# Query, key and value products of chunks 1 and 2 of the first layer, computed during chunk 0's attention and kept in DRAM

## The chip, the cores and the metric

The kernel runs on one core of a Trainium2 chip. A core has TensorE (PE, with its weight loads PEld), VectorE (DVE), ScalarE (ACT), GpSimd (POOL) and SyncE (SP), each with an instruction queue of its own that it works through in order, and 16 DMA engines that all queues share. The metric is the device time of one launch in microseconds, the median of several runs.

## The reference, cut to what matters

Two layers follow each other on 2048 rows of 576 numbers; both use the same weights.

```python
def _A_ref(x, wqkv, wo):               # 32 heads of 18, window W = 8, dilation 2
    qkv = (x @ wqkv) ...               # q, k, v
    idx = pos[:, None] - arange(W) * 2 # each row looks at itself and 7 earlier rows, 2 apart
    logits = q . k[idx] * 18 ** -0.5   # masked where idx < 0
    o = softmax(logits) . v[idx]
    return o @ wo
def _B_ref(x, w1, w2):                 # 576 -> 4608 -> 576
    return silu(x @ w1) @ w2
for layer in range(2):
    x = x + _A_ref(layernorm(x), wqkv, wo)
    x = x + _B_ref(layernorm(x), w1, w2)
```

## The kernel before

The 2048 rows are cut into four chunks of 512 rows. A chunk takes the even or the odd rows (`par`) of one half (`blk`) of the sequence, so that a window lies within rows of one chunk and, for the second half, of the end of the chunk two before it. Within a chunk row 4p+j of it lies in partition p, tile j (NJ = 4 tiles of 128). A step s is one chunk of one layer: s = 0 to 3 are chunks 0 to 3 of layer 0, s = 4 to 7 those of layer 1.

All matrix products take both sides in two float16 halves, a high one and the rest. `passes` (L283) makes 14 matmuls of one product over 576 rows. `front(s)` (L744) makes what comes ahead of the feed-forward of a step:

- `load_x` (L733) loads four x tiles. `layer_norm` (L306) takes statistics on DVE (L311, L312), a Newton inverse root in some 14 small steps (L317 to L327), and scales: on DVE (L335, L340, L294) or, where `on_act` is set, partly on ACT (L343, L346). A DMA transpose on SP (L300) then puts the two halves of each tile into `xa` or `xb`, [128, 9, 512].
- `attention` (L452) goes through four units u of 8 heads. Per unit and tile j PE makes q, k and v at once, 128x432 (L476, called a tile below), and ACT copies them from the `misc` bank into `kv` and `qt` (L480, L482). Four DMAs on ACT's queue copy the halo (L491): the earlier rows that a partition's window needs lie in its neighbours. The edge of a first half is set to zero by POOL (L461, L462), that of a second half is fetched by SP from what POOL saved (L467, L496). DVE multiplies and reduces for the logits (L504, L508, two tiles at a time), does the softmax around the exponential on ACT (L516 to L524, L527), multiplies with the values (L537) and sums over the window (L544, L545).
- `project` (L549) splits o into halves (L558, L294), transposes it into `oT` (L300), multiplies with wo on PE (L573), and adds to x (L580). A second `layer_norm` fills `xb`.

`ffn(s)` (L668) takes the 36 column tiles f of w1. PE makes z (L696, 14 matmuls of 128x512, called a z tile), ACT applies silu and makes the high half of h (L698, L700), DVE the low half (L703). After a group of 6 (step 0) or 9 tiles PE multiplies h with w2 into `acc` (L714; 18 matmuls, called a group, per three f and row tile), and DVE adds it to x (L580).

In step 0 the weights come raw from DRAM: the wqkv columns of a unit (L369), wo (L417), w1 and w2 (L605 to L609), all issued by SP. ACT and DVE scale them and split them into halves (L391 and L394, L438 and L441, L640 to L647), and POOL stores the halves in DRAM (L398, L650, L652), from where later steps load them.

The order of the instructions is not that of the code. Each `op` is given to a planner (L50) with an engine, an assumed duration, the buffers that it needs and a priority; the planner goes through time, and whenever an engine is free it takes the ready operation with the lowest priority number whose buffers are free. Buffers come from tags with a fixed number of slots (L211 to L234), most of them handed out in the order in which the code asks. `after=gate[-1:]` holds the early loads back until chunk 0's first layer norm is done. The attention of a step has priority s - 1, its feed-forward products s + 0.5 and the work around them s - 0.5, so that the attention of step s + 1 is done on DVE and ACT while PE works on the feed-forward of step s. For chunk 0 there is no such feed-forward: its attention, and the splitting of the first weights, stand at the start of the program.

The shared buffer of z on PSUM has two banks, `misc` two, `acc` two.

Of the kernel before, what the change touches and what calls it, by code (L numbers as in the profile page):

```python
# [191 lines left out]
def sliding_attention_silu_ffn(ctx: ExitStack, tc: tile.TileContext, x, wqkv, wo, w1, w2, out):  # L192
# [15 lines left out]
    def T(b):  # L208
# [9 lines left out]
    tag("lg", 2, [P, NJ, W, UH], F32)  # L218
# [5 lines left out]
    tag("oT", 1, [P, 9, P], F16, turns=False)  # L224
    tag("w1", 6, [P, 10, P], F16)
    tag("w2", 11, [P, 2, D], F16)
    tag("h", 11, [P, 2, TB], F16)
    tag("hs", 2, [P, TB], F32)
# [12 lines left out]
           for l in range(NL) for p in range(2) for u in range(NU)}  # L241
# [61 lines left out]

    gate = []

    def layer_norm(xs, prio, into, on_act):  # L306
# [24 lines left out]
        for j in range(NJ):  # L331
# [29 lines left out]
    def raw_wq(u):  # L361
# [3 lines left out]
        for k in range(5):  # L365
# [9 lines left out]
            op("SP", 0.1, load, [], [rs[k]], -9 + u, nbytes=P * 3 * UC * 4, after=gate[-1:] if u > 1 else ())  # L375
# [32 lines left out]
    def raw_wo():  # L408
        rs = [Buf("w2") for _ in range(5)]
        p = -0.7  # L410
        for k in range(5):
# [9 lines left out]
            op("SP", 0.1, load, [], [rs[k]], p, nbytes=P * D * 4, after=gate[-1:])  # L421
# [30 lines left out]
    def attention(s, xT, wq):  # L452
# [4 lines left out]
        for u in range(NU):  # L457
            kv, qt, w = Buf("kv"), Buf("qt"), wq(u)
            if blk == 0:
                def clear(kv=kv):  # L460
                    nc.gpsimd.memset(T(kv)[0:2, 0:3], 0.0)  # L461
                    nc.gpsimd.memset(T(kv)[0:1, 3:7], 0.0)  # L462
                op("POOL", 1.6, clear, [], [(kv, "edge")], pr_)
            else:
# [4 lines left out]
                op("SP", 0.2, edge, [("eds", lay, par, u)], [(kv, "edge")], pr_, nbytes=20000)
            for j in range(NJ):  # L470
                m = Buf("misc")

                def mm(j=j, m=m, w=w):
                    pl = list(passes(lambda k: T(xT)[:, k, j * P:(j + 1) * P], lambda k: T(w)[:, k, :]))
                    for n, (a, b) in enumerate(pl):
                        nc.tensor.matmul(T(m)[:, :3 * UC], a, b, start=n == 0, stop=n == len(pl) - 1)  # L476

                def evac(j=j, m=m, u=u, kv=kv, qt=qt):
                    d = du[:, u:u + 1]
                    nc.scalar.activation(T(kv)[:, j + W - 1].rearrange("p a b -> p (a b)"), T(m)[:, UC:3 * UC],  # L480
                                         AF.Copy, scale=d)
                    nc.scalar.activation(T(qt)[:, j, :], T(m)[:, 0:UC], AF.Copy, scale=d)  # L482
                op("PE", 2.6 if s else 3.9, mm, [(xT, j)] + [(w, k) for k in range(10)], [m], pr_)
                op("ACT", 0.9, evac, [m, ("su", u)], [(kv, j), (qt, j)], pr_)

            def halo(kv=kv):
                t = T(kv)

                for p0, n, i, m in ((0, 112, 3, 4), (112, 15, 3, 4), (0, 112, 0, 3), (112, 14, 0, 3)):
                    d = 1 if i else 2  # L490
                    nc.scalar.dma_start(t[p0 + d:p0 + d + n, i:i + m], t[p0:p0 + n, 11 - m:11])  # L491
            own = [(kv, j) for j in range(NJ)]
            op("ACT", 2.4, halo, own, [(kv, "halo")], pr_ - 0.2, nbytes=P * 14 * UC * 4)
            if blk == 0:
                def save(kv=kv, u=u):
                    nc.gpsimd.dma_start(eds[lay, par, u], T(kv)[P - 2:P, 7:11].rearrange("p a b c -> p (a b c)"))  # L496
# [291 lines left out]
```

## Time and profile before

| | |
|---|---|
| median of 3 runs | 2324.41 us (2321.84 to 2326.78) |
| profiled execution | 2322.78 us |
| its span, first to last instruction | 2321.0 us |
| mean granted TensorE clock | 0.976 |
| busy: PE, DVE, ACT, POOL | 2183.4, 1412.3, 730.5, 96.5 us |
| DMA | 325.42 MB, mean 140 GB/s |
| first z of the program | 238.46 us |

The profile is one execution. Section 1 of its page gives busy time and the number of instructions of each engine, section 2 the same in 40 slices (each digit is the busy share in tenths), section 4 the chain of work that ended last, followed back from the end. A row of a group reads: line, engine, operation, tiles, shapes, count, then busy time in us, mean ns of one, and the idle time of the engine just before them with what ended it. The prediction also uses the chain in order of time (start, length, what), windows (busy time of each engine between two times) and the timeline (start, length, engine, line). A fence of the order shows instructions as they stand in the program on one engine, without times; a name such as kv_79 is one buffer.

### The profile page before, as it was taken

Reading aid. Unit: us, or ns where it says so; the run is one execution under the profiler, and the core shown is the slowest. Engines: PE = TensorE matmul, PEld = TensorE weight load, DVE = VectorE, ACT = ScalarE, POOL = GpSimd, SP = SyncE. Lnnn points to the kernel's source line nnn. Section 1 sums busy time; section 2 is a strip of 40 time slices with the busy share of each in tenths; the row PEclk is TensorE's granted clock in tenths of the full one; section 3 lists DMA queues with packets and bytes.
Section 4 is the critical chain, followed back from the end, with each engine's and each line's share of the span. In section 5 each row is a group of like instructions: output and inputs, shape, how many; then the busy total and the mean of one; then the engine's idle time right before and its main releaser. Section 6 shows DMA issues by size and latency. Waiting matters only on the chain.

```text
span 2321.0 us, 33626 instructions
## 1 busy us (share of the span) xinstructions
PE 2183.4 (94%) x13678; PEld 1344.5 (58%) x13678; DVE 1412.3 (61%) x2120; ACT 730.5 (31%) x1237; POOL 96.5 (4%) x160
## 2 busy tenths in 40 slices
PE   4356899999999999999999999999999999999997
PEld 2123566656666556666666566665566666666665
DVE  6898988639942597346953398426963379521111
ACT  5332577622312332122322323123322223222221
POOL 1100111100000000000000000000000000000000
PEclk9679999999999999999999999999999999999999
DMA  9445567764444553454444644445544543343330
GB/s 260 138 105 135 158 209 216 215 174 143 137 104 153 145 165 111 120 161 125 132 116 133 189 138 138 114 150 129 171 113 117 159 128 109 100 123 126 124 99 27
DMA packets 253340, 325.42 MB, mean 140 GB/s; under 512 B 129680, under 2 KB 160400, under 8 KB 249088
## 3 DMA queue, kind: packets, MB, share of 16 engines
q1 hardware_dynamic: 233728, 254.16, 39.1%
q10 hardware_dynamic: 10048, 32.67, 5.2%
q0 software_dynamic: 9408, 36.43, 4.2%
q8 instruction: 107, 1.75, 0.3%
q14 instruction: 49, 0.40, 0.1%
HBM read 225.79 MB, written 36.42 MB: 113 GB/s over the span
## 4 chain that ended last, share of the span: by engine, by line
PE 46%; issue 40%; DVE 8%; DMA 3%; ACT 1%; POOL 0%; ACTq 0%; SPq 0%; POOLq 0%; DVEq 0%
PE z L696 19%; PE acc L714 18%; PE misc L476 7%; PE acc L573 3%; DVE pr L504 1%; DVE lg L508 1%; DVE pr L537 1%; DVE pr L544 1%; DMA kv<-kv 1%; DMA w<-in_B_w_dram 1%; DMA h<-in_A_wqkv_dram 0%; DMA w<-in_A_wo_dram 0%; DMA oT<-yh 0%; POOL out_dram L729 0%; ACTq L491 0%
## 5 line engine op out<-in xcount | busy, mean ns | idle before, releaser
L696 PE MATMUL z<-xb,w 128*128 128x512 f16 x4032 | 885.0, 380 | 14.7 <-DMA xb<-yh 14.5
L714 PE MATMUL acc<-w,h 128*128 128x288 f16 x6912 | 856.4, 286 | 0.0
L714 PEld LDWEIGHTS <-h 128*128 128x128 f16 x6912 | 676.4, 98 | 177.0
L696 PEld LDWEIGHTS <-w 128*128 128x128 f16 x4032 | 394.9, 98 | 481.7 <-DMA xb<-yh 14.9
L698 ACT ACTIVATE hs<-z,d 128x512 f32<-128x512 f32 x288 | 197.5, 686 | 1015.3 <-PE z L696 996.9
L703 DVE SCALAR_TENSOR_TENSOR h<-hs,sh,h 128x512 f16<-128x512 f32 x288 | 214.5, 749 | 338.7 <-ACT h L700 338.5
L476 PE MATMUL misc<-wq,xa 128*128 128x432 f16 x1792 | 349.0, 357 | 65.4 <-ACT qt L482 52.4
L476 PEld LDWEIGHTS <-xa 128*128 128x128 f16 x1792 | 179.9, 100 | 229.6 <-issue 73.9
L580 DVE SCALAR_TENSOR_TENSOR x<-acc,d,x 128x576 f32<-128x576 f32 x136 | 110.8, 815 | 289.5 <-PE acc L714 289.5
L504 DVE TENSOR_TENSOR pr<-qt,kv 128x2304 f32<-128x2304 f32 x64 | 163.5, 2554 | 116.0 <-ACT qt L482 38.1
L700 ACT ACTIVATE h<-hs,sh 128x512 f16<-128x512 f32 x288 | 207.7, 721 | 9.1
L537 DVE TENSOR_TENSOR pr<-kv,pe 128x1152 f32<-128x1152 f32 x128 | 168.7, 1353 | 1.4
L508 DVE TENSOR_REDUCE lg<-pr 128x128 f32<-128x2304 f32 x64 | 163.2, 2550 | 1.5
L480 ACT ACTIVATE kv<-misc,du 128x288 f32<-128x288 f32 x128 | 63.7, 497 | 239.4 <-PE misc L476 147.3
L544 DVE TENSOR_TENSOR pr<-pr 128x1152 f32<-128x1152 f32 (+1 forms) x128 | 135.1, 1056 | 3.5
L573 PE MATMUL acc<-wo,oT 128*128 128x288 f16 x896 | 116.6, 288 | 12.1 <-DMA oT<-yh 12.1
L573 PEld LDWEIGHTS <-oT 128*128 128x128 f16 x896 | 88.1, 99 | 39.2 <-DMA oT<-yh 13.1
L527 ACT ACTIVATE pe<-lg 128x256 f32<-128x256 f32 x32 | 13.3, 417 | 156.0 <-DVE lg L518 145.7
L580 DVE SCALAR_TENSOR_TENSOR x<-acc,so,x 128x576 f32<-128x576 f32 x32 | 26.1, 817 | 52.8 <-PE acc L573 52.8
L311 DVE BATCH_NORM_STATS2 st<-x 128x6 f32<-128x288 f32 x128 | 52.1, 449 | 9.0 <-DMA x<-in_A_x_dram 8.0
L482 ACT ACTIVATE qt<-misc,du 128x144 f32<-128x144 f32 x128 | 47.8, 374 | 0.0
L729 POOL DMA_DIRECT2D out_dram<-x x16 | 8.7, 542 | 910.4 <-DVE x L580 910.4
(86 smaller groups left out, 764.8 us busy)
## 6 DMA issues: line engine op xcount, KB each, us to landing
w<-w1s SPq DMA_DIRECT2D x252, 320.0 KB, 3.1
w<-w2s SPq DMA_DIRECT2D x252, 288.0 KB, 4.5
wq<-wqs SPq DMA_DIRECT2D x28, 1080.0 KB, 7.2
kv<-kv ACTq DMA_DIRECT2D x32, 504.0 KB, 8.3
kv<-kv ACTq DMA_DIRECT2D x32, 378.0 KB, 6.3
w1s<-w POOLq DMA_DIRECT2D x36, 320.0 KB, 4.0
w<-in_B_w_dram SPq DMA_DIRECT2D x36, 288.0 KB, 4.5
w2s<-w POOLq DMA_DIRECT2D x36, 288.0 KB, 4.0
```

What stands on the lines that cost most here:

```text
L476: nc.tensor.matmul(T(m)[:, :3 * UC], a, b, start=n == 0, stop=n == len(pl) - 1)
L504: nc.vector.tensor_tensor(T(pr), T(qt)[:, j:j + 2, None, :].to_broadcast([P, 2, W, UC]), win(T(kv), j, 2), op=ALU.mult)
L508: nc.vector.tensor_reduce(T(lg)[:, j:j + 2].rearrange("p a w h -> p (a w h)"), T(pr).rearrange("p a w (h d) -> p (a w h) d", d=DH), axis=A ...
L537: nc.vector.tensor_tensor(T(pr)[:, a].rearrange("p w (h d) -> p w h d", d=DH), v, T(pe)[:, j + a, :, :, None].to_broadcast([P, W, UH, DH]) ...
L544: nc.vector.tensor_tensor(t[:, :, 0:h, :], t[:, :, 0:h, :], t[:, :, h:2 * h, :], op=ALU.add)
L573: nc.tensor.matmul(T(acc)[:, h, 0:288], a, b[:, h * 288:(h + 1) * 288], start=n == 0, stop=n == len(pl) - 1)
L580: nc.vector.scalar_tensor_tensor(t, T(acc)[:, :, 0:288], d, t, op0=ALU.mult, op1=ALU.add)
L696: nc.tensor.matmul(T(z), v, u, start=m == 0, stop=m == len(pl) - 1)
L698: op("ACT", 0.7, lambda z=z, hs=hs, f=f: nc.scalar.activation(T(hs), T(z), AF.Silu, scale=d1[:, f:f + 1]), [z, ("s12", f)], [hs], pd, tabl ...
L700: op("ACT", 0.72, lambda hs=hs, h=h, f=f: nc.scalar.activation(T(h)[:, 0, :], T(hs), AF.Copy, scale=shs[i][:, f:f + 1]), [hs, ("sh", i, g) ...
L703: op("DVE", 0.75, lambda hs=hs, h=h, f=f: nc.vector.scalar_tensor_tensor(T(h)[:, 1, :], T(hs), shs[i][:, f:f + 1], T(h)[:, 0, :], op0=ALU. ...
L714: nc.tensor.matmul(T(acc)[:, h, 0:288], T(hb[q])[:, a, j * P:(j + 1) * P], T(wbs[q][0])[:, w, h * 288:(h + 1) * 288], start=q == 0 and m = ...
```

## The change

In layer 0 the query, key and value products of chunks 1 and 2 are made during chunk 0's attention, with the weights that lie in SBUF for chunk 0. Their results go to DRAM tensors `qd`, one for each parity and unit, with seven rows of zeros ahead of the first half. The layer norms of chunks 1 and 2 are made for this ahead of and during chunk 0's attention, into the two `xb` buffers. For two units the weights of chunk 0 are gone when chunk 2 is ready, and are loaded again. The attention of chunks 1 and 2 then fetches keys, values and queries with two DMAs on ACT's queue that read each window's earlier rows from DRAM too, so that they have no products, no copies from PSUM, no halo and no edge of their own. x of chunk 1 is loaded twice.

With this go: one `lg` buffer for two, two `oT` for one, ten `h` for eleven, three `hs` for two (the new copies use `hs` for staging); the raw w1 and w2 loads are issued by POOL and no longer by SP; they and the loads of wo are held back until chunk 1's layer norm is done, and wo and the first two weight tiles get an earlier priority; chunk 0's two layer norms and chunk 1's first are scaled on DVE.

```diff
-    tag("lg", 2, [P, NJ, W, UH], F32)
+    tag("lg", 1, [P, NJ, W, UH], F32)
-    tag("oT", 1, [P, 9, P], F16, turns=False)
+    tag("oT", 2, [P, 9, P], F16, turns=False)
-    tag("h", 11, [P, 2, TB], F16)
-    tag("hs", 2, [P, TB], F32)
+    tag("h", 10, [P, 2, TB], F16)
+    tag("hs", 3, [P, TB], F32)
...
+    QR = 3 * UC
+    qd = [[tc.dram_tile([W - 1 + 2 * TB, QR], F32, name=f"qd{p}{u}") for u in range(NU)] for p in range(2)]
...
+    LATER = 7
...
-    def attention(s, xT, wq):
+    def qkv_matmul(xT, w, j, m):
+        pl = list(passes(lambda k: T(xT)[:, k, j * P:(j + 1) * P], lambda k: T(w)[:, k, :]))
+        for n, (a, b) in enumerate(pl):
+            nc.tensor.matmul(T(m)[:, :3 * UC], a, b, start=n == 0, stop=n == len(pl) - 1)
+
+    def qkv_ahead(c, u, xT, w):
+
+        blk, par = divmod(c, 2)
+        p = -0.95
+        for j in range(NJ):
+            m, g = Buf("misc"), Buf("hs")
+            op("PE", 2.6, lambda j=j, m=m: qkv_matmul(xT, w, j, m), [(xT, j)] + [(w, k) for k in range(10)], [m], p)
+            op("ACT", 0.65, lambda m=m, g=g: nc.scalar.activation(T(g)[:, :QR], T(m)[:, :QR], AF.Copy,
+                                                                  scale=du[:, u:u + 1]), [m, ("su", u)], [g], p)
+            op("POOL", 0.6, lambda j=j, g=g: nc.gpsimd.dma_start(
+                qd_rows(par, u, W - 1 + blk * TB + j, 0, [[NJ * QR, P], [1, QR]]), T(g)[:, :QR]),
+               [g], [("qd", c, u)], p, nbytes=P * QR * 4)
...
+            if wq is None:
+                def fetch(kv=kv, qt=qt, u=u):
+                    row = blk * TB
+                    nc.scalar.dma_start(T(kv).rearrange("p a b c -> p a (b c)"),
+                                      qd_rows(par, u, row, UC, [[NJ * QR, P], [QR, NI], [1, 2 * UC]]))
+                    nc.scalar.dma_start(T(qt), qd_rows(par, u, row + W - 1, 0, [[NJ * QR, P], [QR, NJ], [1, UC]]))
+                op("ACT", 1.4, fetch, [("qd", c, u), ("qd0", u) if blk == 0 else ("eds", lay, par, u)],
+                   own + [(qt, j) for j in range(NJ)] + [(kv, "halo"), (kv, "edge")], pr_, nbytes=P * 4 * UC * 26)
...
-            nc.sync.dma_start(r[:, 0:4, :], w1[0:512, f * P:(f + 1) * P].rearrange("(k p) c -> p k c", p=P))
+            nc.gpsimd.dma_start(r[:, 0:4, :], w1[0:512, f * P:(f + 1) * P].rearrange("(k p) c -> p k c", p=P))
...
-        op("SP", 0.3, load_a, [], [a], prio, nbytes=P * 20 * P, after=gate[-1:])
+        op("POOL", 1.7, load_a, [], [a], prio, nbytes=P * 20 * P, after=gate[LATER:LATER + 1])
...
-                        raw_load(f + q, pd)
-                    ws += raw_split(f, pd)
+                        raw_load(f + q, -0.98 if f < NB else pd)
+                    ws += raw_split(f, -0.98 if f < NB else pd)
...
-        X[s] = load_x(s)
-        xT = layer_norm(X[s], -20.0 if s == 0 else -1.05 if s == 1 else s - 1.0, "xa", s < 2)
-        o = attention(s, xT, raw_wq if s == 0 else (lambda u: load_wq(u, s - 1.0)))
+        X[s] = load_x(s, s - 1.0 if s else -20)
         if s == 0:
+            no_keys()
+            xT = layer_norm(X[0], -20, "xa", False)
+            x1 = layer_norm(load_x(1, -8.5), -8.5, "xb", False)
+            x2 = layer_norm(load_x(2, -2.0), -2.0, "xb", True)
+
+            def more(u, w):
+                qkv_ahead(1, u, x1, w)
+                if u > 1:
+                    qkv_ahead(2, u, x2, w)
+            o = attention(0, xT, raw_wq, more)
+            for u in (0, 1):
+                qkv_ahead(2, u, x2, load_wq(u, -0.95))
             raw_wo()
+        elif s < 3:
+            o = attention(s, None, None)
+        else:
+            o = attention(s, layer_norm(X[s], s - 1.0, "xa", False), lambda u: load_wq(u, s - 1.0))
         project(s, o, X[s])
-        XT[s] = layer_norm(X[s], s - 1.0, "xb", s < 2)
+        XT[s] = layer_norm(X[s], s - 1.0, "xb", s == 1)
```

More of the change, by code (lines that the diff above doesn't have):

```diff
@@ L240, in sliding_attention_silu_ffn, with qd_rows @@
     eds = {(l, p, u): tc.dram_tile([2, NJ * 2 * UC], F32, name=f"ed{l}{p}{u}")
-           for l in range(NL) for p in range(2) for u in range(NU)}
+           for l in range(1, NL) for p in range(2) for u in range(NU)}
+    QR = 3 * UC
+    qd = [[tc.dram_tile([W - 1 + 2 * TB, QR], F32, name=f"qd{p}{u}") for u in range(NU)] for p in range(2)]
+    def qd_rows(par, u, row, col, dims):
+        t = qd[par][u]
+        return bass.AP(tensor=t.tensor, offset=t.offset + row * QR + col, ap=dims)
     def x_rows(t, c, j):
@@ L374, in square @@
                                      accum_out=accq[:, u, k:k + 1])
-            op("SP", 0.1, load, [], [rs[k]], -9 + u, nbytes=P * 3 * UC * 4, after=gate[-1:] if u > 1 else ())
+            op("SP", 0.1, load, [], [rs[k]], -9 + u, nbytes=P * 3 * UC * 4, after=gate[3:4] if u > 1 else ())
             op("ACT", 0.8, square, [rs[k]], [("accq", u, k)], -9 + u)
@@ L409, in raw_wo @@
         rs = [Buf("w2") for _ in range(5)]
-        p = -0.7
+        p = -1.02
         for k in range(5):
@@ L420, in square @@
                 nc.scalar.activation(junk[:, :D], r(k), AF.Square, accum_out=acco[:, k:k + 1])
-            op("SP", 0.1, load, [], [rs[k]], p, nbytes=P * D * 4, after=gate[-1:])
+            op("SP", 0.1, load, [], [rs[k]], p, nbytes=P * D * 4, after=gate[LATER:LATER + 1])
             op("ACT", 0.9, square, [rs[k]], [("acco", k)], p)
@@ L450, in win, with no_keys, fn, attention @@
         return bass.AP(tensor=v.tensor, offset=v.offset, ap=[v.ap[0], [2 * UC, n], [-2 * UC, W], [1, UC]])
-    def attention(s, xT, wq):
+    def qkv_matmul(xT, w, j, m):
[13 more added lines that the diff above has]
+               [g], [("qd", c, u)], p, nbytes=P * QR * 4)
+    def no_keys():
+        g = Buf("hs")
+        op("POOL", 0.5, lambda: nc.gpsimd.memset(T(g)[0:W - 1, :QR], 0.0), [], [g], -20)
+        def fn():
+            for u in range(NU):
+                nc.gpsimd.dma_start(qd_rows(1, u, 0, 0, [[QR, W - 1], [1, QR]]), T(g)[0:W - 1, :QR])
+        op("POOL", 2.2, fn, [g], [("qd0", u) for u in range(NU)], -20, nbytes=50000)
+    def attention(s, xT, wq, more=None):
         lay, c = divmod(s, NC)
@@ L470, in attention @@
[L470 to L496, printed above, removed]
-                op("POOL", 0.6, save, own, [("eds", lay, par, u)], pr_, nbytes=20000)
+            kv, qt = Buf("kv"), Buf("qt")
```

71 lines of the change are left out of this document (53 added, 18 removed).

## Prediction

> **What bounds the kernel now.** I read the page first, then the chain of waits in order of time, then windows cut where the stages meet, then groups by line. The page:
>
> ```profile
> span 2321.0 us, 33626 instructions
> PE 2183.4 (94%) x13678; PEld 1344.5 (58%) x13678; DVE 1412.3 (61%) x2120; ACT 730.5 (31%) x1237; POOL 96.5 (4%) x160
> PE   4356899999999999999999999999999999999997
> DVE  6898988639942597346953398426963379521111
> ```
>
> Each digit is 58 us. PE is partly idle in the first four slices and at 9 after that: a head of about 238 us in which PE waits, and then a PE-bound rest. The chain in order of time (start, length, what):
>
> ```profile
> 253.26 5.11 PE misc L476 x28
> 442.19 3.02 PE z L696 x14
> 460.46 17.64 PE acc L714 x144
> 478.10 24.17 PE z L696 x112
> 502.27 25.55 PE misc L476 x140
> 548.49 10.22 PE misc L476 x56
> 576.59 5.11 PE misc L476 x28
> ```
>
> From 478.10 the chain is PE alone, and the query/key/value products (L476) stand on it: a tile of 14 matmuls costs 25.55/10 = 2.555 us, a z tile 3.02, an acc group of 18 matmuls 17.64/8 = 2.205. Now the stages:
>
> ```profile
> 0.00:51.60 51.60, 22.15 (x96) 10.84 (x97) 28.90 (x110) 30.37 (x71) 6.05 (x12) 0.90 0.93 249
> 51.60:173.00 121.40, 55.27 (x236) 26.58 (x234) 111.16 (x138) 47.46 (x107) 12.21 (x17) 0.71 0.47 135
> 173.00:238.46 65.46, 36.87 (x221) 22.09 (x219) 57.63 (x89) 14.99 (x29) 5.09 (x8) 0.87 0.53 129
> 238.46:300.00 61.54, 61.54 (x344) 34.32 (x345) 58.53 (x86) 40.97 (x72) 11.03 (x19) 0.96 0.62 193
> 300.00:360.00 60.00, 60.00 (x413) 40.04 (x412) 48.96 (x94) 43.21 (x81) 9.71 (x18) 1.00 0.57 189
> ```
>
> The columns after the length are busy time on PE, PEld, DVE, ACT and POOL, then clock, DMA share and GB/s. 51.6 is chunk 0's first attention multiply, 173.0 its last sum, 238.46 the first z. DVE is busy 111 of 121 us in the middle stretch, PE 55: DVE sets the head, and PE has 238.46 - 22.15 - 55.27 - 36.87 = 124 us free there.
>
> **What is removed.** The two tiles at 253.26 (chunk 1's last; its other 14 lie in the head already) and the 16 tiles of chunk 2 at 502.27, 548.49 and 576.59: 5.11 + 25.55 + 10.22 + 5.11 = 45.99 us of PE work leaves the PE-bound part. Of this 40.88 us leaves chunk 1's feed-forward, where nothing but PE is on the chain. What was hidden there, the halo copies and two ACT evacuations per tile, goes too, at no gain. So the ceiling is 46 us unless the head itself becomes shorter.
>
> **What is added to the head.** PE gets 18 tiles more: 18 x 2.555 = 46 us warm. A tile in the head can cost more:
>
> ```profile
> 65.22 4.83 PE misc L476 x14
> ```
>
> At 4.83 us each they would be 87 us, still under 124; I take the warm price, because the tiles now stand in long runs. Each also needs an ACT copy, a POOL store and one of three staging buffers; ACT's copies stand behind its fetches of chunk 1's keys, which wait until DVE is done with a kv buffer, so a late DVE holds PE there too.
>
> DVE pays for chunk 2's layer norm, moved into chunk 0's attention. In the order of VectorE, first the start of that attention before, where L504/L508 are multiply and reduction:
>
> ```order
> L504 TENSOR_TENSOR pr_88<-qt_81,kv_79 128x2304
> L508 TENSOR_REDUCE lg_84<-pr_88 128x128
> L504 TENSOR_TENSOR pr_88<-qt_81,kv_79 128x2304
> L508 TENSOR_REDUCE lg_84<-pr_88 128x128
> L516 TENSOR_TENSOR lg_84<-lg_84,mrow 128x256
> L517 TENSOR_REDUCE mx_89<-lg_84 128x32
> ```
>
> and the same place on VectorE now (L561/L565 are these two; x_70 to x_73 hold chunk 2):
>
> ```order
> L561 TENSOR_TENSOR pr_87<-qt_81,kv_79 128x2304
> L565 TENSOR_REDUCE lg_84<-pr_87 128x128
> L321 BN_STATS st_126<-x_70 128x6 x2
> L322 BN_AGGR mv_128<-st_126 128x2
> L321 BN_STATS st_126<-x_71 128x6 x2
> L322 BN_AGGR mv_128<-st_126 128x2
> L321 BN_STATS st_126<-x_72 128x6 x2
> L322 BN_AGGR mv_128<-st_126 128x2
> L321 BN_STATS st_126<-x_73 128x6 x2
> L322 BN_AGGR mv_128<-st_126 128x2
> L327 TENSOR_SCALAR nt_130<-mv_128 128x4
> ```
>
> Between the first multiply and the last sum of chunk 0 the new order holds, beyond the old: 8 statistics, 4 aggregates, 16 small steps of the inverse root, 5 weight splits of wq and 4 of w2 (the later loads push these in), and some fewer scale steps. Their prices:
>
> ```profile
> L311 DVE BATCH_NORM_STATS2 st<-x 128x6 f32<-128x288 f32 x128 | 52.1, 449 | 9.0 <-DMA x<-in_A_x_dram 8.0
> L312 DVE BATCH_NORM_AGGREGATE mv<-st 128x2 f32<-128x12 f32 x64 | 13.4, 209 | 2.2
> L323 DVE TENSOR_SCALAR nt<-nt 128x4 f32<-128x4 f32 x48 | 8.2, 170 | 1.6
> L394 DVE SCALAR_TENSOR_TENSOR wq<-h,su,wq 128x432 f16<-128x432 f32 x20 | 12.1, 661 | 9.6 <-ACT wq L391 9.6
> L647 DVE SCALAR_TENSOR_TENSOR w<-w,s,w 128x576 f16<-128x576 f32 x36 | 28.5, 812 | 1.4 <-ACT w L645 1.2 <-issue 0.2
> ```
>
> 8 x 0.449 + 4 x 0.209 + 16 x 0.17 + 5 x 0.661 + 4 x 0.812 = 13.7, less about 1 for the scale steps: **+13 us** if DVE idles as much as before (10 of 121 us), +3 if the new work fills all that idling, +23 if the longer waits for POOL and DMA double it. I take 13. The first multiply stays near 51.6: chunk 1's whole layer norm now stands before it on DVE, about 9 us of work more, but DVE had 51.6 - 28.9 = 23 us idle there, and what released it, the halo copy of the keys, still waits for the same loads.
>
> Then the projection. In the order of SyncE, which issues the transposes, the end of chunk 0 before (oT is the transposed attention output, xb the input of the feed-forward):
>
> ```order
> L300 DMA_TRANSPOSE oT0_95<-yh0_93 128x9x128
> L609 DMA w28_110<-in_B_w2_dram 128x576
> L404 DMA wq1_78<-wqs3_231 128x4320
> L609 DMA w25_107<-in_B_w2_dram 128x576
> L300 DMA_TRANSPOSE oT0_95<-yh1_94 128x9x128
> L300 DMA_TRANSPOSE oT0_95<-yh0_93 128x9x128
> L300 DMA_TRANSPOSE oT0_95<-yh1_94 128x9x128
> L404 DMA wq0_77<-wqs0_228 128x4320
> ```
>
> and on SyncE now:
>
> ```order
> L309 DMA_TRANSPOSE oT0_94<-yh0_92 128x9x128
> L309 DMA_TRANSPOSE oT1_95<-yh1_93 128x9x128
> L413 DMA wq1_78<-wqs1_229 128x4320
> L309 DMA_TRANSPOSE oT0_94<-yh0_92 128x9x128
> L309 DMA_TRANSPOSE oT1_95<-yh1_93 128x9x128
> L413 DMA wq0_77<-wqs0_228 128x4320
> L309 DMA_TRANSPOSE xb0_75<-yh0_92 128x9x128
> L309 DMA_TRANSPOSE xb0_75<-yh1_93 128x9x128
> L309 DMA_TRANSPOSE xb0_75<-yh0_92 128x9x128
> L413 DMA wq1_78<-wqs1_229 128x4320
> L309 DMA_TRANSPOSE xb0_75<-yh1_93 128x9x128
> ```
>
> The transposes alternate between two oT, so two are under way at once. From the timeline before (start, length):
>
> ```profile
> 184.54 21.47 SPq L300 DMA_TRANSPOSE oT<-yh  x3
> 220.11 0.16 DVE L329 TENSOR_SCALAR nt<-mv 128x4 f32<-128x4 f32 x1
> ```
>
> Each transpose waited until PE had read the only oT: the last three took from 184.54 to 206.01, 7.2 us each, and the whole stretch from 173.0 to 238.46 is 65.5 us. Now four steps of about 7 plus 3.5 us (transpose, product) shrink to two rounds of about 11, some 25 us after the last sum instead of 38; and DVE has only 40 instead of 56 us of work in this stretch (the rows between, times the prices by operation), though it now does the layer norm's scaling that ACT did, because one attention unit of chunk 1 has moved behind the first z. With the layer norm after it (18 us before and after, counted from the end of the inverse root at 220.3 to 238.46) I get 47 to 48 us: **-18 us**. At worst it is -8: the last load of wq stands ahead of the last xb transpose, and waits for the last of six tiles that PE runs after the projection; at 4.83 us each instead of 2.555 that is up to 14 us later, of which 4 are covered.
>
> So the first z comes at 238.5 + 13 - 18 = 233.5 (bounds: 238.5 + 3 - 18 = 223 and 238.5 + 23 - 8 = 253, the latter only if both go wrong).
>
> **Chunk 0's feed-forward** took 478.10 - 238.46 = 239.6 us. It loses 5.1 us of tiles. But more of chunk 1's attention, and of the splits, is left to DVE between the first z and chunk 1's projection. The prices:
>
> ```profile
> L504 DVE TENSOR_TENSOR pr<-qt,kv 128x2304 f32<-128x2304 f32 x64 | 163.5, 2554 | 116.0 <-ACT qt L482 38.1 <-DMA kv<-kv 37.9 <-ACT kv L480 37.5
> L508 DVE TENSOR_REDUCE lg<-pr 128x128 f32<-128x2304 f32 x64 | 163.2, 2550 | 1.5
> L537 DVE TENSOR_TENSOR pr<-kv,pe 128x1152 f32<-128x1152 f32 x128 | 168.7, 1353 | 1.4
> L544 DVE TENSOR_TENSOR pr<-pr 128x1152 f32<-128x1152 f32 (+1 forms) x128 | 135.1, 1056 | 3.5
> L545 DVE TENSOR_TENSOR o<-pr 128x288 f32<-128x288 f32 x64 | 29.3, 458 | 2.2
> L517 DVE TENSOR_REDUCE mx<-lg 128x32 f32<-128x256 f32 x32 | 19.6, 614 | 1.1
> L642 DVE SCALAR_TENSOR_TENSOR w<-w,s,w 128x640 f16<-128x640 f32 x36 | 31.6, 881 | 6.9 <-ACT w L640 6.7
> L580 DVE SCALAR_TENSOR_TENSOR x<-acc,so,x 128x576 f32<-128x576 f32 x32 | 26.1, 817 | 52.8 <-PE acc L573 52.8
> ```
>
> Two multiplies and two reductions (4 x 2.55), a softmax head (about 1.5 with its maximum of 0.61), one weighted product with its sums (1.35 + 2 x 1.06 + 0.46), six splits (2 x 0.88 + 4 x 0.81), four updates of x (4 x 0.82), one h (0.75) and some 15 small steps of 0.17 come to 27 us more. PE reaches the projection 27 z tiles and 32 groups after the first z: 27 x 3.02 + 32 x 2.205 = 152 us. DVE took 139 us from 235 to the first transpose of that projection (L300 at 374.45), now 139 + 27 = 166, less up to 11 us of idling (60 - 48.96 in the window from 300):
>
> ```profile
> 374.45 1.34 SPq L300 DMA_TRANSPOSE oT<-yh  x1
> ```
>
> With a start 4 us before z and 7 us of transpose PE waits 166 - 11 - 4 + 7 - 152 = 6 us at best for DVE, 17 at worst; I take 8. In this stage, therefore: -5.1 + 8 = **+3 us** (0 to +12).
>
> **Chunk 1's feed-forward** loses 40.9 us. Chunk 2's attention loses its cover with the tiles: PE reaches its projection 18 z tiles and 16 groups after the stage begins, 54 + 35 = 90 us. By the rows left and the same prices DVE has some 96 us to do from its last h of chunk 0 on, which stands six groups (13 us) before that stage begins, and 7 us of transpose follow. **+2 us** (0 to 6). From chunk 2 on the order of PE is the same but for where the projections stand. One lg for two, ten h for eleven and three hs for two cost nothing there: between a reduction and the next one that needs lg lies a multiply of 2.55 us, and a group needs nine h.
>
> **Loads on POOL.** The raw feed-forward weights are now issued by POOL: four more DMAs per tile of weights, besides two stores.
>
> ```profile
> L650 POOL DMA_DIRECT2D w1s<-w x36: 539/539/560, 93.8 to 453.5; - x36
> ```
>
> At 0.54 us six are 3.2 us per weight tile against 6.65 us (239.6/36) that PE gives one: hidden. The 512-row load has no row here; from 0.54 to four times that (four times the rows) it stays hidden, 4.9 us. The Trainium skill, "SBUF — State Buffer", section "SBUF: two separate sides", speaks against this move: a DMA issued from GpSimd cannot write its descriptors while VectorE runs an operation that holds both ports. By its example, 0.62 us becoming 3.1, six would take an estimated 18.6 us. The row above, 560 ns at most beside a VectorE that is nearly always busy, does not show it.
>
> **The sum.** -5 (first z) + 3 - 40.9 + 2 = -41 us. The profiled execution is 2322.78 us (1.78 around its span), 1.6 below the median of 2324.41. 2322.8 - 41 = 2281.9, as a median 2283.5.
>
> **Rivals.**
> 1. The head and chunk 0's feed-forward give much of it back: DVE was full there, and one unit of attention more behind the first z means PE waits at two projections without tiles to fill in. For it: DVE is busy 58.5 of 61.5 us behind the first z. Against: the idling from 300. Price: first z at 253, +12 and +6, so -8 at most: 2304 to 2316. Chance 0.11.
> 2. The head gets shorter still, as DVE fills its idling: first z at 223, no wait in the feed-forward: -15.5 - 5 - 40.9 = -61: 2263. Chance 0.07.
> 3. Slower: POOL's DMAs are held up, as VectorE works beside them. It decides from 6.65/6 = 1.1 us per DMA on; at 1.5 us each weight tile takes 9 us, and 36 of them (9 - 6.65) x 36 = +85 us in chunk 0's feed-forward, 2283 + 85 = 2368. Against it the 539 to 560 ns. This is how the skill's rule would act. Chance 0.04.
> 4. Nothing happens, because chunk 2's products were hidden: the chain speaks against it, as they stand on it alone. 0.01.
>
> The forecast has 0.77.
>
> **The numbers.** 2283; the range from 2266 to 2305 leaves out the end of rival 2, most of rival 1 and rival 3. About 0.2% (5 us) is what a measurement of this kernel can tell from no change. Faster by more: 0.93, same 0.02 (the end of rival 1 and rival 4), slower 0.05.
>
> **What would show it.** Right: the first z near 234; 16 tiles gone from the chain after chunk 0's feed-forward; PE waits of some us for oT in it; POOL's DMAs at 0.54. Wrong: a first z behind 250 with PE or ACT waiting for staging buffers; PE waiting for w from DRAM; POOL's DMAs above 1 us.

## The result, and the profile after

The median of four runs is **2289.09 us** (2287.28 to 2291.1), beside 2323.58 us for the kernel before (four runs, 2321.84 to 2326.78): a ratio of 0.985, with a 95% interval from 0.9833 to 0.9867, or 34.5 us less. The profiled execution took 2288.33 us, against 2322.78.

The page of the changed kernel, whose rows answer to those shown of the kernel before:

```profile
span 2286.5 us, 33537 instructions
PE 2184.0 (96%) x13678; PEld 1345.2 (59%) x13678; DVE 1415.1 (62%) x2134; ACT 718.5 (31%) x1193; POOL 192.5 (8%) x329
...
PE   4479799899999999999999999999999999999998
...
DVE  6898999799513697138952598426972379611111
```

PE does the same work as before (2184.0 and 2183.4 us). It is now fuller in the third and fourth slice (7 and 9 instead of 5 and 6), and idle for moments in the fifth, into which the first z falls, and in the eighth, in chunk 0's feed-forward. The chain of the changed kernel in order of time, from the end of chunk 0's feed-forward to the start of chunk 2's:

```profile
473.62 17.64 PE acc L771 x144
491.26 27.20 PE z L753 x126
518.45 26.46 PE acc L771 x216
...
719.60 24.17 PE z L753 x112
```

The same start of chunk 2's feed-forward in the kernel before:

```profile
747.32 24.17 PE z L696 x112
```

No query/key/value product (L464 now) stands in that stage any more. It took 747.32 - 478.10 = 269.22 us and takes 719.60 - 491.26 = 228.34: exactly the 40.88 us of 16 tiles. The windows cut where the stages meet (59.40 is the first multiply, 193.15 chunk 0's last sum, 246.03 the first z; columns as in the prediction):

```profile
0.00:59.40 59.40, 28.11 (x120) 14.08 (x121) 37.00 (x133) 25.07 (x65) 14.89 (x27) 0.91 0.99 222
59.40:193.15 133.75, 92.27 (x441) 46.39 (x441) 122.62 (x172) 57.62 (x119) 32.11 (x56) 0.86 0.64 185
193.15:246.03 52.88, 38.93 (x241) 24.06 (x240) 47.68 (x78) 7.95 (x13) 5.94 (x11) 0.90 0.72 205
246.03:300.00 53.97, 52.86 (x302) 29.79 (x302) 50.03 (x76) 35.67 (x57) 26.92 (x47) 0.97 0.63 212
```

Three stages ahead of the first z took 51.6, 121.4 and 65.5 us and take 59.4, 133.8 and 52.9, so the first z comes 7.6 us later than before, at 246.03. Chunk 0's feed-forward takes 245.2 us (239.6). Together: +7.6 + 5.6 - 40.9 = -27.7 us, and this difference stays to the last store (2309.19 before, 2281.47 now). The other 6.7 us of the span lie behind that store, 6.4 of them in POOL's closing drain (a DRAIN instruction at the end of its queue, the longest of three). Its rows, first of the kernel before, then of the changed one:

```profile
L784 POOLq DRAIN  x3: 40/102/10764, 2309.2 to 2320.7; - x3
```

```profile
L855 POOLq DRAIN  x3: 40/93/4327, 2281.4 to 2286.3; - x3
```

Where the head lost time is seen in three places of the changed kernel. VectorE, in the timeline, sat idle before the first multiply for the halo copies of the keys, and behind it for chunk 2's x:

```profile
59.40 2.56 DVE L561 TENSOR_TENSOR pr<-qt,kv 128x2304 f32<-128x2304 f32 x1 [11.22 <-DMA kv<-kv]
...
69.81 0.82 DVE L321 BATCH_NORM_STATS2 st<-x 128x6 f32<-128x288 f32 x2 [5.26 <-DMA x<-in_A_x_dram]
```

The DMA share is 0.99 over these first 59.4 us. The statistics of chunk 2 stand in VectorE's queue ahead of the second multiply, so their wait is that of the attention. (The x that they wait for is loaded once more for chunk 2's own step, as that of chunk 1 is: the profile has 24 such loads for 16.) Then SyncE, ahead of the first z:

```profile
227.00 9.29 SPq L309 DMA_TRANSPOSE xb<-yh  x3
236.39 0.52 SPq L413 DMA_DIRECT2D wq<-wqs  x1
237.50 1.87 SPq L309 DMA_TRANSPOSE xb<-yh  x1
```

A weight load of 1.08 MB, which nothing needs before chunk 3, goes out just ahead of the last transpose of `xb`, and z at 246.03 comes 8.5 us after that transpose was issued; in the kernel before it was 3.2 us. And in chunk 0's feed-forward, on the chain:

```profile
395.60 7.12 DMA w<-in_B_w_dram
402.73 13.46 DMA oT<-yh
```

PE's waits for oT add up to 6.0 us there.

### The profile page after: what moved, and what is told of

It reads as the page before. It is cut to its first block, busy times and chain, and to the rows that moved or that the text cites. A ratio compares the mean times of both kernels' runs of the same rounds, so it can differ in the third digit from the quotient of the medians.

```text
span 2286.5 us, 33537 instructions
## 1 busy us (share of the span) xinstructions
PE 2184.0 (96%) x13678; PEld 1345.2 (59%) x13678; DVE 1415.1 (62%) x2134; ACT 718.5 (31%) x1193; POOL 192.5 (8%) x329
## 4 chain that ended last, share of the span: by engine, by line
PE 45%; issue 41%; DVE 8%; DMA 3%; SPq 1%; POOL 1%; ACT 1%; ACTq 0%; POOLq 0%; DVEq 0%
PE z L753 19%; PE acc L771 18%; PE misc L464 5%; PE acc L630 3%; DVE pr L594 1%; DVE pr L561 1%; DMA x<-in_A_x_dram 1%; DMA oT<-yh 1%; DVE pr L601 1%; DVE lg L565 1%; DMA xb<-yh 1%; DVE yh L303 0%; POOL out_dram L786 0%; DMA kv<-kv 0%; SPq L795 0%
## 5 line engine op out<-in xcount | busy, mean ns | idle before, releaser
L753 PEld LDWEIGHTS <-w 128*128 128x128 f16 x4032 | 394.8, 98 | 480.8 <-issue 13.3
L464 PE MATMUL misc<-wq,xa 128*128 128x432 f16 x1344 | 258.6, 354 | 14.9 <-ACT qt L532 5.0
L464 PEld LDWEIGHTS <-xa 128*128 128x128 f16 x1344 | 134.3, 100 | 135.8 <-issue 26.3
L630 PEld LDWEIGHTS <-oT 128*128 128x128 f16 x896 | 88.9, 99 | 36.3 <-DMA oT<-yh 10.4
L530 ACT ACTIVATE kv<-misc,du 128x288 f32<-128x288 f32 x96 | 47.7, 497 | 186.9 <-PE misc L464 120.6
L464 PE MATMUL misc<-wq,xb 128*128 128x432 f16 x448 | 88.9, 360 | 15.1 <-ACT qt L532 7.2
L464 PEld LDWEIGHTS <-xb 128*128 128x128 f16 x448 | 45.4, 101 | 57.7 <-issue 23.3
L584 ACT ACTIVATE pe<-lg 128x256 f32<-128x256 f32 x32 | 13.3, 416 | 118.1 <-DVE lg L575 111.2
```

The source lines that it names most:

```text
L630: nc.tensor.matmul(T(acc)[:, h, 0:288], a, b[:, h * 288:(h + 1) * 288], start=n == 0, stop=n == len(pl) - 1)
L753: nc.tensor.matmul(T(z), v, u, start=m == 0, stop=m == len(pl) - 1)
```

## The experiments

Every kernel was timed beside the kernel before on the same chip (2322.5 to 2323.9 us in the three groups). The table has the marks by which each is read: the first attention multiply, the last sum of chunk 0's attention, the first z, the first z of chunk 2's feed-forward, and the median. From the fourth mark to the last store all of them took 1562 to 1564 us, so whatever differs was decided before it.

| | first multiply | last sum | first z | chunk 2's first z | median us | ratio to before |
|---|---|---|---|---|---|---|
| before | 51.6 | 173.0 | 238.5 | 747.3 | 2323.58 | |
| the change | 59.4 | 193.2 | 246.0 | 719.6 | 2289.09 | 0.9833 to 0.9867 |
| e1_chunk1_only | 63.4 | 198.5 | 238.9 | 750.6 | 2320.71 | 0.9982 to 1.0000 |
| e2_no_norm2 | 63.1 | 200.5 | 259.7 | 740.8 | 2308.26 | 0.9917 to 0.9950 |
| e3_loads_on_sync | 56.9 | 191.3 | 247.6 | 733.9 | 2299.50 | 0.9883 to 0.9916 |
| e4_one_oT | 60.4 | 191.8 | 250.1 | 742.5 | 2313.20 | 0.9944 to 0.9976 |
| e5_loads_later | 54.9 | 182.7 | 239.6 | 719.5 | 2289.29 | 0.9837 to 0.9870 |
| e6_norm2_small | 60.5 | 189.0 | 242.1 | 715.2 | 2286.64 | 0.9818 to 0.9859 |
| e7_before_two_oT | 51.5 | 170.4 | 234.2 | 753.6 | 2330.89 | 1.0021 to 1.0043 |
| e8_both_later | 56.0 | 177.3 | 227.9 | 709.8 | 2276.07 | 0.9783 to 0.9812 |
| e9_norm2_later | 59.9 | 216.7 | 263.8 | 746.0 | 2312.73 | 0.9942 to 0.9972 |
| e10_before_two_oT_held | 51.3 | 172.5 | 227.4 | 744.6 | 2321.63 | 0.9981 to 0.9999 |
| e11_change_held | 59.9 | 192.2 | 241.6 | 720.7 | 2289.86 | 0.9838 to 0.9871 |
| e12_all_three | 55.8 | 176.3 | 222.1 | 691.6 | 2262.77 | 0.9726 to 0.9755 |

### e1_chunk1_only: the 16 tiles put back

```diff
...
-            x2 = layer_norm(load_x(2, -2.0), -2.0, "xb", True)
...
-                if u > 1:
-                    qkv_ahead(2, u, x2, w)
...
-            for u in (0, 1):
-                qkv_ahead(2, u, x2, load_wq(u, -0.95))
...
-        elif s < 3:
+        elif s < 2:
```

> Only chunk 1's queries, keys and values are computed ahead and kept in DRAM; chunk 2's layer norm and 16 products stand in chunk 1's feed-forward again, as before the change. Everything else (two oT, loads of the feed-forward weights on POOL, storage of the keys) stays. Theory (the gain is the 16 tiles of chunk 2, 40.9 us of PE work, that left a stage in which PE alone is on the chain, less what the head pays for chunk 2's layer norm): chunk 1's feed-forward is back at 269 us, the first multiply back near 52 and the first z 8 to 15 us earlier than 246; the time is 2289 + 41 - (8 to 15) = 2315 to 2322. Rival (the gain comes from the head's new arrangement, and the tiles of chunk 2 were covered): the time stays within 8 us of 2289.

2320.71 us, inside the theory's range. The chain of this kernel, at the starts of chunk 1's and of chunk 2's feed-forward:

```profile
481.40 24.17 PE z L753 x112
...
750.62 24.17 PE z L753 x112
```

Chunk 1's feed-forward takes 269.22 us again, to the hundredth what it took before the change. So the gain is chunk 2's 16 tiles; the rival falls. But the head did not get shorter in the way that the theory said. The first z comes 7.1 us earlier, yet the first multiply and the last sum came later than with the change, though VectorE had less to do. Its waits up to the last sum (the longer one for kv, 14.9 us, ends with the first multiply; the others lie between it and the last sum, and e2 below has the same two):

```profile
DVE pr L561 <- DMA kv<-kv: 24.6, 2, 14.9
DVE mx L579 <- ACT pe L584: 9.4, 2, 8.9
```

### e2_no_norm2: chunk 2's layer norm left out of the head

```diff
-            x2 = layer_norm(load_x(2, -2.0), -2.0, "xb", True)
...
-                    qkv_ahead(2, u, x2, w)
+                    qkv_ahead(2, u, x1, w)
...
```

> Chunk 2's layer norm with its four loads and four transposes is left out of the head, and chunk 2's products are made from chunk 1's normed input, so PE, ACT and POOL do the same work (the output is not the reference's: chunk 2 gets chunk 1's queries, keys and values). Theory (chunk 2's layer norm on VectorE, some 10 us of work, stands on the head's path): the last sum of chunk 0 comes 10 to 13 us earlier (180 to 183 instead of 193), the first z near 234, the time 2277 to 2280. Rival (the ten tiles that PE runs last before the projection, 25.7 us on the chain, would hold it anyway): the first z moves by under 4 us, the time is 2285 to 2289.

2308.26 us: 19 us slower with less work, outside of what either expected. From the first multiply to the last sum it took 137.4 us (133.8 with the change), with VectorE busy for 113.1 (122.6), so that it stood idle for 24.3. The planner had moved other work into the gap. ACT's timeline shows what:

```profile
75.93 0.68 ACT L429 ACTIVATE junk<-w 128x576 f16<-128x576 f32 x1 [10.88 <-DMA w<-in_A_wo_dram]
...
81.19 0.48 ACT L530 ACTIVATE kv<-misc,du 128x288 f32<-128x288 f32 x1
...
81.70 3.40 ACTq L542 DMA_DIRECT2D kv<-kv  x4
```

The squares of wo stand in ACT's queue ahead of the last copy of keys, of the halo copies and of the exponential behind these, and waited 10.9 us for their load, which SyncE had issued behind chunk 1's transposes. VectorE waited 10.6 us for that exponential. Its other long wait, 10.2 us for the halo copies of the last unit, ended at 175.88, and begins in ACT's queue too:

```profile
159.93 0.40 ACTq L500 DMA_DIRECT2D kv<-qd  x1
...
161.45 0.50 ACT L530 ACTIVATE kv<-misc,du 128x288 f32<-128x288 f32 x1 [6.51 <-issue]
```

The fetch of chunk 1's keys needs a kv buffer, which VectorE had in use until 159.85, and ACT's copies of the last unit's keys stand behind it. This is the hold-up that the prediction named, "a late DVE holds PE there too". Taking an operation out says little about its price where a planner fills the hole anew.

### e3_loads_on_sync: the raw feed-forward weights issued by SyncE again

```diff
...
-            nc.gpsimd.dma_start(r[:, 0:4, :], w1[0:512, ...
+            nc.sync.dma_start(r[:, 0:4, :], w1[0:512, ...
...
-        op("POOL", 0.6, lambda: nc.gpsimd.dma_start(fl(T(b).bitcast(F32)), w2[...
+        op("SP", 0.1, lambda: nc.sync.dma_start(fl(T(b).bitcast(F32)), w2[...
```

> The raw feed-forward weights are issued by SyncE again, as before the change; all else is the change. Theory A (issued by POOL, they run beside the halo copies of the keys and the transposes and slow them: the first multiply at 59.4 instead of 51.6, the transposes of chunk 1's oT in the feed-forward landing 13.5 us after issue): the first multiply is near 52, the wait of PE for oT in chunk 0's feed-forward falls below 3 us, the time is 2277 to 2285. Theory B (the same bytes cross the same DMA engines in either queue, and SyncE's queue holds the loads behind its transposes): no gain, the first multiply stays beyond 57, PE or ACT wait longer for w from DRAM in chunk 0's feed-forward, the time is 2289 to 2300.

2299.50 us, ten more than the change: theory B by the time, though the first multiply came at 56.9, 2.5 us earlier, halfway to theory A. PE did not wait for oT in chunk 0's feed-forward, as A had it, but 14.8 us for chunk 1's `xb` at its end. The chain there:

```profile
486.32 9.19 DMA w<-w2s
...
497.46 5.19 DMA xb<-yh
```

The transposes of chunk 1's `xb` stand in SyncE's queue behind a load that is late itself. So moving these loads to POOL was worth 10 us, the different order that the planner then made included.

### e4_one_oT: one oT in the changed kernel

```diff
-    tag("oT", 2, [P, 9, P], F16, turns=False)
+    tag("oT", 1, [P, 9, P], F16, turns=False)
```

> One oT instead of two, all else is the change. Theory (two transposes under way at once shorten both the projection stretch of chunk 0 and chunk 1's projection): from chunk 0's last sum to the first z 60 to 66 us instead of 52.9, and PE waits some 10 us more for oT in chunk 0's feed-forward; the time is 2300 to 2310. Rival (the transposes share one set of DMA engines and go one after the other anyway): the stretch grows by under 3 us, the time is 2287 to 2292.

2313.20 us, above the theory's 2300 to 2310. From the last sum to the first z it took 58.4 us instead of 52.9, a little below the theory's 60; chunk 0's feed-forward lost more than expected. With the planner's order shifted, PE's waits for oT were 7.9 us there, and two late weight loads stood on the chain:

```profile
461.97 6.94 DMA w<-in_B_w_dram
...
470.55 10.58 DMA w<-in_B_w_dram
```

The direction is the theory's; how much of the 24 us is the buffer and how much the new order isn't told apart.

After these four a second theory stood against the prediction's own view, that VectorE's amount of work sets the head: full DMA engines, and queues that stand behind late transfers, set it.

### e5_loads_later: the raw loads wait for chunk 2's layer norm

```diff
-        ... nbytes=P * 20 * P, after=gate[LATER:LATER + 1])
+        ... nbytes=P * 20 * P, after=gate[11:12])
```

> The first loads of the raw feed-forward weights wait for chunk 2's layer norm instead of chunk 1's, so 2.3 MB leave the stretch from 45 to 70 us, in which the DMA engines are full; the planner's order around them shifts a little (the first projection of chunk 1 stands later among the z tiles). Theory 2, formed after the first four runs (the head's first 90 us are set by full DMA engines and by what queues in order behind late transfers, not by the amount of VectorE work): the first multiply comes at 53 to 56 instead of 59.4, VectorE's statistics of chunk 2 wait under 3 us for x instead of 7.1, the time is 2275 to 2284. Rival (VectorE's work sets the head): the last sum of chunk 0 stays within 3 us of 193, the time is 2286 to 2293.

The head does what theory 2 says: the first multiply at 54.9, no wait of the statistics for x, the last sum 10.4 us earlier, the first z 6.4 us earlier. The time doesn't: 2289.29 us, where theory 2 had 2275 to 2284. The chain at the end of chunk 0's feed-forward:

```profile
460.88 15.45 PE acc L771 x126
...
476.77 4.30 SPq L309
...
481.18 7.29 DMA xb<-yh
...
488.56 1.44 PE z L753 x3
```

PE ran out of work there, and waited 10 us for chunk 1's `xb`. With the loads' new times the planner had put chunk 1's projection later among the z tiles (two z tiles and eight groups lie between its last product and chunk 1's feed-forward, against six and 16 in the change), too late to cover the layer norm behind it. The gain was given back in the next stage.

### e6_norm2_small: less work on VectorE in an unchanged order

```diff
-                    nc.vector.bn_stats(T(st)[:, j, h, :], T(xs[j])[:, h * 288:(h + 1) * 288])
+                    nc.vector.bn_stats(T(st)[:, j, h, :], T(xs[j])[:, h * 288:h * 288 + (16 if small else 288)])
...
+            if small:
+                nc.vector.tensor_scalar(r, T(mv)[:, :, 1], LNS, None, op0=ALU.mult)
+                nc.vector.tensor_scalar(a, T(mv)[:, :, 0], -1.0, None, op0=ALU.mult)
+                return
```

> The order of every engine is kept, but VectorE's share of chunk 2's layer norm is cut to 16 columns and two small steps, some 7 us of its 9.5 us of work gone (chunk 2's normed input is not the reference's). Rival (VectorE's work sets the head): the last sum of chunk 0 comes 6 to 8 us earlier than 193, the time is 2281 to 2283. Theory 2 (late transfers and the queues behind them set it): VectorE's idle time grows by as much as the work shrinks, the last sum moves by under 3 us, the time is 2286 to 2290.

The window from the first multiply to the last sum:

```profile
60.54:188.99 128.45, 88.72 (x441) 45.41 (x441) 115.60 (x154) 57.16 (x119) 32.04 (x56) 0.89 0.64 191
```

VectorE's work shrank by 122.6 - 115.6 = 7.0 us, and the stretch by 133.8 - 128.5 = 5.3; the first multiply happened to come 1.1 us later. But one execution does not fix this gain. In e4 and e11 VectorE's order up to the last sum is that of the change, instruction by instruction, and there the stretch took 131.4 and 132.4 us:

```profile
60.41:191.78 131.37, 89.70 (x441) 45.79 (x441) 122.72 (x172) 57.79 (x119) 31.86 (x56) 0.87 0.63 187
```

So of 7.0 us less work 2.9 to 5.3 come out as time. The last sum came 4.2 us earlier, between the two expectations: VectorE's work is paid for in part, and the waits for transfers are paid for too. The median, 2286.64 us, is 2.5 us below that of the change, and its runs span more than that (2280.14 to 2291.48).

### e7_before_two_oT and e10_before_two_oT_held: the buffers alone

e7 is the kernel before with the buffer counts of the change:

```diff
...
-    tag("oT", 1, [P, 9, P], F16, turns=False)
+    tag("oT", 2, [P, 9, P], F16, turns=False)
...
```

> The kernel before, with nothing of the change but its buffer counts: two oT, one lg, ten h, three hs. Theory (two transposes under way shorten the projection stretch): from chunk 0's last sum to the first z 52 to 57 us instead of 65.5, the first z at 226 to 231, the time 2308 to 2315. Rival (the buffers are worth something only together with the products ahead): the stretch stays over 62 us, the time is 2319 to 2326. The closing drain of POOL, 10.8 us before and 4.3 us after, should stay near 10.8 if it belongs to the kernel before rather than to one execution.

2330.89 us, slower than the kernel before; from the last sum to the first z still 63.8 us. On its chain the fourth update of x comes at 199.36, where it came at 215.37; 2.7 of these 16 us were there at the last sum already, so two transposes at a time did save some 13 us. SyncE's timeline shows where they went:

```profile
209.13 8.22 SPq L300 DMA_TRANSPOSE xb<-yh  x3
220.45 0.33 SPq L404 DMA_DIRECT2D wq<-wqs  x1
220.88 1.31 SPq L300 DMA_TRANSPOSE xb<-yh  x1
```

The last transpose stands behind chunk 2's first weight load. That load waited for PE's tiles until 220.45, and the transpose, issued behind its 1.08 MB, let z start only at 234.20, 13.3 us later. e10 holds the load back:

```diff
...
+    hold.append(turned[-1])
...
-           nbytes=P * 60 * UC)
+           nbytes=P * 60 * UC, after=hold if prio > 0.5 else ())
```

> The kernel before with the buffer counts of the change (e7_before_two_oT), and chunk 2's first load of query/key/value weights (1.08 MB on SyncE) held until the last transpose of chunk 0's feed-forward input, where in e7 it stood ahead of it, waited for PE's tiles, and the transpose then landed 13.3 us after its issue. Theory (two oT do save some 15 us in the projection, and that load gave them back): the last transpose lands within 5 us, the first z at 221 to 226 instead of 234.2, the time 2318 to 2324 (feed-forward of chunk 0 as in e7, 250 us). Rival (the transpose is slow for its own sake): the first z stays over 231, the time over 2327.

```profile
211.13 11.55 SPq L300 DMA_TRANSPOSE xb<-yh  x4
222.77 0.53 SPq L404 DMA_DIRECT2D wq<-wqs  x1
```

The transposes are through, the stretch is 54.9 us instead of 63.8, the first z comes at 227.4 (1.4 us later than expected, behind PE's own tiles), and the time is 2321.63 us, in the theory's range. So two oT are worth about 10 us in this stretch, but only with the load out of the way; and here, too, most of it is lost again in chunk 0's feed-forward, which takes 248.0 us instead of 239.6 (PE waits 6.9 us there for ACT's silu).

### e8_both_later and e9_norm2_later: chunk 2's layer norm behind the attention

```diff
-            x2 = layer_norm(load_x(2, -2.0), -2.0, "xb", True)
+            x2 = layer_norm(load_x(2, -2.0), -0.97, "xb", True)
```

e9 has this alone, e8 this and the later loads of e5.

> Loads as in e5_loads_later, and chunk 2's layer norm ranks behind chunk 0's attention in the planner, so its statistics no longer stand between the first two multiplies on VectorE, where they waited 7.1 us for x. Theory 2: the first multiply at 53 to 56, the last sum of chunk 0 at 178 to 186; but chunk 2's products start later and pile up before the first z; the time is 2268 to 2284. Rival (the products ahead set the end of the head): the first z stays beyond 244, the time is 2286 to 2296.

> The change, with chunk 2's layer norm ranked behind chunk 0's attention in the planner; the raw loads stay where the change has them (the other half of e8_both_later). Theory 2 (late transfers and the queues behind them set the head; the statistics on VectorE waited 7.1 us for x between the first two multiplies): the first multiply stays at 59 to 61, the last sum of chunk 0 at 184 to 188 instead of 193, the first z 5 to 9 us earlier than 246, the time 2280 to 2286. Rival (only both together free anything, since what follows the statistics waits for the second halo copy as in e2_no_norm2): the last sum beyond 191, the time 2287 to 2300.

e8: 2276.07 us, 13 less than the change, with the time and the first multiply as theory 2 has them and the last sum, at 177.3, just ahead of its range. e9: 2312.73 us, slower than the change, as its rival said and worse. VectorE did as much work there between the first multiply and the last sum as in the change (122.5 and 122.6 us), but stood idle for 34.3 us, most of it ahead of the last unit:

```profile
192.06 2.56 DVE L561 TENSOR_TENSOR pr<-qt,kv 128x2304 f32<-128x2304 f32 x1 [19.78 <-DMA kv<-kv]
```

PE's timeline shows why the keys of that unit came late:

```profile
113.69 0.59 PE L688 MATMUL misc<-accw,ones 128*128 128x4 f32 x2 [5.04 <-ACT qt L532]
157.18 3.04 PE L464 MATMUL misc<-wq,xb 128*128 128x432 f16 x8 [42.90 <-DVE p L286]
```

L688 adds up the squares of raw weights in a `misc` bank, and VectorE reads the sum (L286). The sums made at 97.75 and 113.69 were read only at 156.98 and 158.05, because the reading stood in VectorE's queue behind the attention. With a sum in each of the two banks PE had none for its tiles and stood idle for 42.9 us; then it ran six tiles of later chunks ahead of the last unit's four, and that unit's halo copies went out at 185.85. In e8, with the loads later, these sums begin at 137 instead of 67, no wait of PE between the first multiply and the last sum is above 7.6 us, and the same edit gains.

### e11_change_held and e12_all_three: the weight loads of chunk 3 held

The edit of e10, in the changed kernel (e11), and together with those of e8 (e12).

> The change, with chunk 3's first two loads of query/key/value weights held in the same way; in the change one of them stands ahead of the last transpose, which lands 8.5 us after its issue. Theory: the last transpose lands within 5 us, the first z at 239 to 243 instead of 246, the time 2282 to 2286. Rival (VectorE's attention of chunk 1, not the first z, sets the end of chunk 0's feed-forward): the first z moves as said, the feed-forward grows by as much, the time 2287 to 2291.

> e8_both_later and the held loads together. Theory: the first z at 222 to 226 instead of 227.9, the time 2270 to 2274. Rival (chunk 1's attention on VectorE sets the end of chunk 0's feed-forward by now): the feed-forward's start of chunk 1 stays within 2 us of 479, the time 2275 to 2279.

e11: the first z 4.5 us earlier, as expected, and 2289.86 us: the rival. Chunk 0's feed-forward took the gain back. On its chain stands a transpose of oT that landed late, and PE's waits were longer:

```profile
394.30 15.08 DMA oT<-yh
```

```profile
PE acc L630 <- DMA oT<-yh: 7.1, 1, 7.1
```

PE waited 7.1 us for oT (6.0 in the change) and 3.8 for split weights (1.9), and the same matmuls took 2.4 us longer, at a granted clock of 0.97 instead of 0.99.

e12: **2262.77 us**, 26 below the change and 61 below the kernel before, and better than its own theory. Its stages, up to the start of chunk 1's feed-forward at 463.21:

```profile
0.00:55.82 55.82, 26.44 (x110) 13.21 (x111) 36.83 (x133) 24.87 (x65) 8.29 (x16) 0.91 0.99 225
55.82:176.27 120.45, 87.92 (x426) 44.14 (x424) 117.03 (x152) 52.41 (x108) 35.31 (x60) 0.89 0.64 193
176.27:222.11 45.84, 43.67 (x266) 26.19 (x266) 41.53 (x88) 13.74 (x25) 8.78 (x16) 0.95 0.80 210
222.11:463.21 241.10, 233.01 (x1511) 147.08 (x1512) 227.31 (x386) 158.18 (x274) 105.13 (x183) 1.00 0.75 233
```

The first z comes 23.9 us earlier than in the change, and chunk 0's feed-forward takes 4.1 us less: with six z tiles and eight groups between chunk 1's projection and its feed-forward, PE's waits for oT are 0.3 us, and it does not wait for `xb`. Alone, the three edits gained 0, lost 24 and lost 1 us; together they gain 26.

## Why the prediction was right, and where its steps were not

The forecast was 2283, the result 2289.09. The direction is right, and so is the mechanism of the largest term, the tiles that leave chunk 1's feed-forward. The head came out with the wrong sign: the first z was to come 5 us earlier and came 7.6 later. Of the 34.5 us, 27.7 lie in the stages that the forecast added up, where it had 41; another 6.4 come from a closing drain that it did not know of. That these bring the result nearer to the forecast is luck; without them it would have been about 2295.5, still inside the range.

1. **Chunk 1's feed-forward, -40.9 + 2**: the first term is exact (-40.88), and e1 shows that the gain hangs on it. The 2 us of stall did not come; chunk 2's attention was done in time.
2. **"The first multiply stays near 51.6"**: this step failed, by +7.8 us. The prediction counted VectorE's idle time as cover for chunk 1's layer norm, and said that the halo copy "still waits for the same loads". It was issued 2.4 us later (from 43.99 on, before from 41.61) and took 5.4 us longer until VectorE could start (15.4 us, before 10.0). In e5, with the raw loads later, the first multiply comes 4.5 of the 7.8 us earlier, and in e3, with the loads in SyncE's queue, 2.5. The rest was not taken apart; chunk 1's four transposes stood on SyncE from 38.5 to 54.8, and no run took these away.
3. **+13 us of VectorE work in the attention**: measured +12.3 (133.75 against 121.4), with 11.5 us more work and 0.9 us more idle time; in e4 and e11, with the same order, +10.0 and +11. e6 confirms it in part: 7.0 us of work less are 2.9 to 5.3 us of time less. Under it lie 7.1 us of waiting for x that the prediction did not name, since it looked at VectorE's queue and not at when the loads would land. PE's 18 tiles more cost what was taken (46): PE was busy for 159.3 us ahead of the first z, before for 114.3.
4. **-18 us in the projection stretch**: measured -12.6. The mechanism holds (e10: 54.9 us with two oT and nothing else of the change). The loss is the one that the prediction named as its worst case, "the last load of wq stands ahead of the last xb transpose", only not by PE's tiles but by the load's own bytes: e11, with the load held, has the last transpose used after 4.7 us instead of 8.5, and the first z 4.5 us earlier. So the first z came at 246.0 instead of 233.5, inside the bounds of 223 to 253.
5. **Chunk 0's feed-forward, +3**: measured +5.6, with 6.0 us of waiting for oT where 8 were taken.
6. **Loads on POOL hidden**: right. The rows of the changed kernel for the 512-row load, the two of 64 rows and the one of w2:

```profile
L662 POOL DMA_DIRECT2D w<-in_B_w_dram x36: 754/762/818, 45.0 to 436.4; - x36
```

```profile
L664 POOL DMA_DIRECT2D w<-in_B_w_dram x72: 527/536/587, 45.8 to 437.6; - x72
```

```profile
L666 POOL DMA_DIRECT2D w<-in_B_w_dram x36: 537/542/606, 48.6 to 455.0; - x36
```

   With the two stores a weight tile costs POOL 0.76 + 2 x 0.54 + 0.54 + 2 x 0.55 = 3.5 us, against 6.8 that PE gives one. The 3.1 us per DMA that the Trainium skill, "SBUF — State Buffer", section "SBUF: two separate sides", has beside a copy on VectorE do not appear: the longest of these is 0.82 us, and VectorE is busy for 221.9 of the 245.2 us of chunk 0's feed-forward. Rival 3 falls. Which of VectorE's operations here hold both ports, if any, no run shows.
7. **Not foreseen: the closing drain of POOL**, 6.4 us shorter. It belongs to the kernels and not to one execution: 10.76 us in the kernel before, in e7 and in e10, 3.4 to 4.3 in the changed kernel and the ten made from it. Which part of the change shortens it was not tried; it is not the loads' queue, since e3 has 4.32.

Of the errors, the first z alone is +12.5, chunk 0's feed-forward +2.6, the stall -2, and the drain -6.4: +6.7, about the distance of 2288.33 from 2281.9.

## What to carry to other kernels

Work moved out of a stage where one engine is alone on the chain is worth its full length there; what it costs in the stage that takes it in depends on the order in which it stands in the queues, and could not be read from the idle time that the receiving engine shows. In a queue that is worked through in order, look for what stands behind an instruction that waits for a transfer: statistics ahead of a multiply, squares ahead of an exponential, the reading of a sum that keeps a PSUM bank from PE, a weight load that nobody needs yet ahead of the last transpose. And where a planner sets the order, one such edit alone can shift the stall to the next stage or make it longer, so try the edits together before calling one of them useless.

## What the runs showed of the hardware that was not expected

- A DMA transpose of [128, 9, 128] halves was landed and used 3.2 us after its issue in the kernel before (from 235.24), but 8.5 us behind a load of 1.08 MB in the change and 13.3 us in e7. Holding the load brought e11 to 4.7 us.
- POOL's DMA with four pieces of 128 rows took 0.76 us to issue, beside 0.54 for one piece: 40% more for four times the rows.
- POOL's last drain took 10.76 us in every kernel with the old code and 3.4 to 4.3 in every one with the new, with nothing else at work in the core's last microseconds but the last store, which lands 2.4 us after its issue. Why stays open.
